# Attention and a mixture of experts in one program: the order of attention's work placed by a list of tasks

## The chip, the cores and the metric
The kernel runs on one core of a Trainium2 chip. The metric is the device time of one execution in microseconds (us). The core's engines are TensorE (PE in the profile, with its weight loads as PEld), VectorE (DVE), ScalarE (ACT), GpSimd (POOL) and SyncE (SP), which only issues transfers. Each engine runs its own queue of instructions strictly in order; an instruction waits in its queue until what it needs has been signalled by others, and everything behind it on that engine waits too.

## The reference
Attention with a bias that a small network computes from the positions, then a mixture of eight experts in which each token goes to its best expert.

```python
B, H, S, D = q.shape                      # 2, 8, 576, 64
scores = np.matmul(q, k.transpose(0, 1, 3, 2)) / np.sqrt(D)
x = (np.log1p(np.abs(rel)) / psi_i)[..., None]        # of the positions alone
bias = np.maximum(x @ w1 + b1, 0.0) @ w2              # hidden 32, one value per head
scores = scores + bias.transpose(2, 0, 1)[None]       # the same for both batches
attn = np.exp(scores - scores.max(-1, keepdims=True))
attn = attn / (attn.sum(-1, keepdims=True) + 1e-09)
x = np.matmul(attn, v)                    # laid out as 1152 tokens x 512
logits = x @ w_gate                       # 8 experts
# each token goes to its argmax expert, at most 288 tokens each, in order
y = np.maximum(x_e @ w1[e], 0.0) @ w2[e]  # 512 -> 1024 -> 512, for each expert
out[token] = gate_w[token] * y            # gate_w: softmax probability; 0 if not kept
```

## The kernel before
**Units.** Attention is cut into 40 units, numbered in the order in which they run. A unit is a batch, a tile t of query rows (t = 0 to 3 of 128 rows, t = 4 of 64) and a pair of heads; four units in a row make a tile. Batch 0 runs its tiles 4, 3, 2, 1, 0 (units 0 to 19), batch 1 its tiles 0 to 4 (units 20 to 39). For a unit, `scores` multiplies queries and keys on TensorE into two PSUM buffers `s`, one for each head (L211, L218 for t = 4). `softmax` adds the bias tile `bt` and takes the row minimum of the negated sum on VectorE (L223, output `ed`, minimum `mn`), then the exponential with its row sum on ScalarE (L227). Two units later (LAG = 2) `transp_rem` and `transp` turn the exponentials around on TensorE (L235): the last 64 columns (the remainder) into free corners of a later unit's `s`, the rest into the one PSUM buffer `tt`. Copies bring them to SBUF: the remainder `rt` (L266) and, in two halves, `at` (L248 on ScalarE, L250 on VectorE). `attn_v` (L289) multiplies them with the values into `av`. After a tile, `tile_a` copies `av` to `xT` (L303) and `tile_b` multiplies by a matrix that turns it back and applies the gate (L326), then scales by the row sums on VectorE (L329 to L346) and stores the rows `x` to DRAM.

**Bias blocks.** The bias is computed once, in 36 blocks of 16 query rows, for tiles 4, 3, 2, 1, 0 in turn. For each block, `hidden` makes four tiles `hid` (on VectorE L147, ScalarE L145 or GpSimd L143), `bias_block` multiplies them on TensorE (L166) into `tt`, `s` or `pt` and writes the block out of PSUM in two pieces, `bo` (L175 on VectorE, L177 on ScalarE). The block is stored to DRAM (L180, on SP's or ScalarE's queue) and read back skewed as bias tiles `bt`, of which four are kept (L193, L196, SP's queue). So batch 0's units run beside the bias blocks, batch 1's alone.

**Experts.** After batch 0 its tokens are routed (`group_a`, `group_b`, `pick`), and the first expert's rows of batch 0 are gathered (`match`, `fetch`, index products at L420). Its weights are loaded and split into a high and a low half (`wh` L85, L87, `wl` L90). `step(0, 0..9)`, its input transposes (L624) and eight halves of layer 1 (L633), are put between the units of batch 1. Layer 2 (L657), the second expert and a small part of a third follow attention.

**What sets the order.** One loop over slots n, a unit each, emits the program. TensorE's queue is the order of emission (`manual_schedule` with `MANF`). On the other engines a scheduler of the framework orders the instructions when the program is built, by its own estimates and priorities. In a slot, `attn_v` comes for two units at a time in every second slot, then two bias blocks, the scores, and the transposes:

```python
        for u in ([n - 4, n - 3] if n % 2 == 0 and 4 <= n <= NU else [NU - 2, NU - 1] if n == NU + 1 else []):
            attn_v(u)
        for z in range(2):
            bias_block()
            for c in range(4):
                hidden()
        new = scores(n) if n < NU else []
```

Which engine makes which hidden tile, bias output and transpose copy stands in tables, `P["h"]`, `P["e"]` and `P["t"]`; bias blocks with an odd number use `tt`.

## Time and profile before

| | |
|---|---|
| median of 3 runs | 352.01 us (351.0 to 352.93) |
| the profiled execution | 350.3 us |
| its span, first to last instruction | 348.3 us |
| TensorE busy | 273.7 us, 79% of the span |
| VectorE, ScalarE, GpSimd busy | 200.2, 169.2, 87.9 us |
| TensorE's granted clock, mean | 0.929 of full (2.4 GHz) |
| moved by DMA | 59.84 MB |

An engine's busy time counts the instructions that it executes, not the waits between them; a matmul that is held up inside a group counts as busy. The granted clock of a stretch is a mean over two levels, 2.4 and 1.2 GHz.

### The profile page before, as it was taken

How to read it: one execution, taken by the hardware profiler on the slowest of the kernel's cores; microseconds unless marked ns; L12 is line 12 of the kernel's file. 1: busy time of each engine (PE TensorE's matmuls, PEld its weight loads, DVE VectorE, ACT ScalarE, POOL GpSimd, SP SyncE). 2: the span in 40 equal slices, each digit the busy share in tenths (PEclk: the TensorE clock that was granted, in tenths of full speed). 3: DMA queues.
4: the chain of work that ended last, by engine and by line, in shares of the span. 5: the costliest groups of instructions: out<-in, count | busy, mean ns of one | idle time of the engine just before them, and what ended most of it. 6: DMA issues, size and time to landing. Idle time of an engine off the chain costs nothing.

```text
span 348.3 us, 7329 instructions
## 1 busy us (share of the span) xinstructions
PE 273.7 (79%) x2801; PEld 205.7 (59%) x2801; DVE 200.2 (57%) x625; ACT 169.2 (49%) x348; POOL 87.9 (25%) x79
## 2 busy tenths in 40 slices
PE   4795675767697788787886977898897969799891
PEld 2222343444355356565664755787777959799880
DVE  5897479566655444553669654366478586661010
ACT  4575546716546555445555455465432453651230
POOL 1359285126411010000000670122122240300031
PEclk9999899898969899999999896999998787999997
DMA  6999675741274229646645884252003799200011
GB/s 202 359 307 357 209 281 190 292 154 70 86 272 152 107 58 347 237 135 206 201 138 162 312 286 153 91 134 88 2 23 117 271 323 390 73 2 0 3 48 36
DMA packets 27627, 59.84 MB, mean 172 GB/s; under 512 B 3812, under 2 KB 5348, under 8 KB 27584
## 3 DMA queue, kind: packets, MB, share of 16 engines
q1 hardware_dynamic: 24384, 51.97, 44.4%
q10 hardware_dynamic: 2304, 4.84, 3.6%
q0 software_dynamic: 896, 2.47, 2.5%
q8 instruction: 24, 0.39, 0.5%
q14 instruction: 19, 0.16, 0.1%
HBM read 42.57 MB, written 16.99 MB: 171 GB/s over the span
## 4 chain that ended last, share of the span: by engine, by line
PE 34%; issue 17%; ACT 11%; DVE 11%; POOL 2%; POOLq 0%; ACTq 0%
PE av L289 10%; PE s L211 9%; ACT ed L227 6%; ACT at L248 4%; DVE ed L223 3%; PE tt L235 3%; PE pt L633 3%; PE tt L166 2%; PE pt L326 2%; POOL out_dram L643 1%; DVE rt L266 1%; PE pt L657 1%; DVE x L346 1%; PE pt L420 1%; PE s L218 1%
## 5 line engine op out<-in xcount | busy, mean ns | idle before, releaser
L227 ACT ACTIVATE ed<-ed,mn 128x576 f32<-128x576 f32 x72 | 55.3, 769 | 28.2 <-DVE mn L223 26.6
L143 POOL TENSOR_SCALAR hid<-c_u,nbv 128x304 f32<-128x304 f32 (+14 forms) x32 | 46.8, 1474 | 59.9 <-PE tt L166 31.6
L248 ACT COPY at<-tt 128x512 f32<-128x512 f32 x62 | 35.2, 575 | 53.8 <-PE tt L235 51.9
L211 PE MATMUL s<-kraw,q 64*128 64x288 f32 x256 | 51.2, 463 | 7.0 <-DVE mn L223 5.0
L289 PE MATMUL av<-at,vt 128*64 128x128 f32 (+1 forms) x576 | 45.0, 281 | 13.6 <-ACT at L248 7.7
L223 DVE CUSTOM_DVE_ANT_0 ed<-s,bt 128x576 f32<-128x576 f32 x72 | 51.5, 748 | 0.0
L147 DVE TENSOR_SCALAR hid<-c_u,c_v 128x496 f32<-128x496 f32 (+17 forms) x86 | 41.2, 532 | 17.0 <-PE tt L166 16.9
L289 PEld LDWEIGHTS av<-at,vt 128*64 128x64 f32 x576 | 35.8, 142 | 18.4 <-ACT at L248 10.0
L211 PEld LDWEIGHTS s<-kraw,q 64*128 64x128 f32 x256 | 27.5, 202 | 26.8 <-issue 11.1
L166 PE MATMUL tt<-hid,c_w2bd 128*32 128x512 f32 (+17 forms) x176 | 24.4, 532 | 18.9 <-ACT at L248 14.8
L266 DVE COPY rt<-s 128x64 f32<-128x64 f32 (+1 forms) x80 | 14.2, 216 | 36.3 <-PE s L235 35.0
L90 POOL TENSOR_TENSOR wl<-raw,wh 128x1024 fp32r<-128x1024 f32 x8 | 18.8, 2356 | 50.7 <-ACT wh L85 37.4
L85 ACT CAST wh<-raw 128x1024 fp32r<-128x1024 f32 x20 | 20.6, 1048 | 19.1 <-DMA raw<-in_w_dram 13.0
L235 PE MATMUL tt<-c_ident,ed 64*128 64x64 f32 x576 | 27.3, 230 | 2.5 <-DVE bo L175 0.8
L235 PEld LDWEIGHTS tt<-c_ident,ed 64*128 64x128 f32 x576 | 22.9, 143 | 8.5 <-ACT at L248 4.2
L633 PE MATMUL pt<-xh,wh 128*128 128x288 f32 x64 | 19.8, 309 | 5.5 <-ACT y L642 1.3
L145 ACT ACTIVATE hid<-c_u,c_v 128x528 f32<-128x528 f32 (+14 forms) x26 | 16.6, 673 | 14.9 <-PE tt L166 8.0
L90 DVE TENSOR_TENSOR wl<-raw,wh 128x1024 fp32r<-128x1024 f32 x16 | 19.5, 1219 | 6.0 <-ACT wh L85 6.0
L166 PEld LDWEIGHTS tt<-hid,c_w2bd 128*32 128x32 f32 x176 | 5.8, 114 | 28.0 <-ACT at L248 15.5
L657 PE MATMUL pt<-hh,wh 128*128 128x288 f32 x64 | 21.0, 329 | 0.0
L657 PE MATMUL pt<-hh,wl 128*128 128x288 f32 x64 | 20.5, 320 | 0.0
L657 PE MATMUL pt<-hl,wh 128*128 128x288 f32 x64 | 20.4, 319 | 0.0
(172 smaller groups left out, 503.9 us busy)
## 6 DMA issues: line engine op xcount, KB each, us to landing
bt<-bd SPq DMA_DIRECT2D x28, 576.0 KB, 5.1
raw<-in_w_dram SPq DMA_DIRECT2D x24, 512.0 KB, 4.9
bd<-bo SPq DMA_DIRECT2D x20, 295.5 KB, 2.6
bd<-bo ACTq DMA_DIRECT2D x16, 295.5 KB, 3.9
vt<-in_v_dram SPq DMA_DIRECT2D x8, 320.0 KB, 4.9
kraw<-in_k_dram SPq DMA_DIRECT2D x8, 288.0 KB, 5.6
bt<-bd SPq DMA_DIRECT2D x8, 288.0 KB, 4.4
out_dram<-y SPq DMA_DIRECT2D x3, 768.0 KB, 10.0
```

What stands on the lines that cost most here:

```text
L90: (nc.vector if eng[1] == "d" else nc.gpsimd).tensor_tensor(lo, raw, hi.bitcast(F32), op=ALU.subtract)
L143: nc.gpsimd.tensor_scalar(hid[:, :m], wu[:, :m], nbv[:, w:w + 1], None, op0=ALU.max)
L147: nc.vector.tensor_scalar(hid[:, :m], wu[:, :m], bvw[:, w:w + 1], 0.0, op0=ALU.add, op1=ALU.max)
L166: nc.tensor.matmul(ps[32 * c:32 * c + 32, lo:hi], lhsT=w2bd, rhs=hids[n, c][:, lo:hi], start=True, stop=True, tile_position=(0, 32 * c))
L211: nc.tensor.matmul(ps[i][:, r, :HALF], lhsT=q[p, hp], rhs=k[p, r * HALF:(r + 1) * HALF], start=True, stop=True, tile_position=(64 * i, 0))
L223: nc.vector.tensor_tensor_reduce(out=ed.rearrange("p (r j) -> p r j", r=2), in0=ps[:, :, :HALF], in1=bias.rearrange("p (r j) -> p r j", r= ...
L227: nc.scalar.activation(ed, ed, AF.Exp, scale=-1.0, bias=mn, accum_out=total)
L235: nc.tensor.transpose(out[r][:w], ed[p, o:o + w], ident[p, p], tile_position=(64 * r, 0))
L248: nc.scalar.copy(o, v)
L289: nc.tensor.matmul(o, lhsT=lh, rhs=rh, start=(j == 0), stop=(j == 4), tile_position=(0, r))
L633: nc.tensor.matmul(ph[:, :cap], lhsT=u[:, k], rhs=x[:, k], start=(k + z == 0), stop=(k == 3 and z == 2))
L657: nc.tensor.matmul(py[:, :cap], lhsT=w, rhs=hx, start=(f + i == 0), stop=(f == 7 and i == 2))
```

## The change
The loop over slots, the tables `P` and the calls at slots go. In their place attention, the routing and the first expert's part inside it are described as some 800 tasks. A task has the engines that may do it, a duration for each, the tasks that must end before, a rank, and the buffers that it takes with the tasks that give them back. `place_tasks` takes, of the tasks that can start first (or within 0.3 us of it), the one with the lowest rank, gives it the engine that ends it soonest and, where there is a choice, the PSUM buffer that is free soonest, and emits its instructions. All engines' queues now follow this order through attention. Behind it a short list, in the order of before, emits the rest, with TensorE alone in the order of emission.

To that end the functions are cut in pieces that are tasks of their own (matmul, output and store of a bias block; minimum and exponential; transposes and their copies; the pieces of `tile_b`, `group_a`, `group_b`, `pick` and layer 1). All bias stores go to SP's queue. Pools grow: `hid` from 13 to 16 buffers, `sm` from 3 to 4, `vr` from 2 to 4. In a bias block one hidden tile is always GpSimd's and another may be, and odd and even blocks share `pt` and `tt`.

```diff
-    hp_p = brest.enter_context(tc.tile_pool(name="hid", bufs=13, side="right"))
+    hp_p = brest.enter_context(tc.tile_pool(name="hid", bufs=HB, side="right"))
...
-    P = {
-        "h": ['daad', 'dddd', 'daad', 'daad', 'daad', 'dadp', 'dadp', 'dadd', 'dapp', 'daad', 'dddd',
...
-        "e": 'dadddaadaaadaaaddaadaaaddaadaadaadaa',
...
+    def bias_psum(n):
+        return ("s", "tt") if n < 4 else ("tt",) if span(blocks[n]) > 512 else ("pt", "tt")
...
+    def turned_rem(n, eng):
+        m = 128 if units[n][1] < 4 else 64
+        rt = ats[n, 1] = atp.tile([128, 128], F32, name="rt")
+        for r, z in enumerate(rps.pop(n)):
+            (nc.scalar.copy if eng == "a" else nc.vector.tensor_copy)(rt[:m, 64 * r:64 * r + 64], z[:m])
...
+    man = ExitStack()
+    man.enter_context(tc.manual_schedule(engines={ET.PE, ET.DVE, ET.Activation, ET.Pool, ET.SP}))
...
+    bufs = {"hid": HB, "bo": BB, "s": 2, "tt": 1, "pt": 1, "av": 1, "bt": 4, "q": 3, "v": 4, "vr": 4, "ed": 4, "at": 4,
+            "rt": 4, "mn": 4, "sums": 4, "xT": 2, "x": 2, "raw": 3}
+    after_us = {"e": 0.3, "d": 0.12, "a": 0.15, "p": 0.2, "s": 2.3}
...
+    def place_tasks(start):
+        free_at = dict(start)
+        ends, held, left = {}, {}, dict(tasks)
+        while left:
+            best = []
+            for name, (engines, us, fn, after, rank, takes, late) in left.items():
+                if any(a not in ends for a in after):
+                    continue
+                ready = max([ends[a] for a in after], default=0.0)
...
+                if len(chosen) == len(takes):
+                    e = min(engines, key=lambda e: (max(free_at[e], ready) + us[e], e))
+                    best.append((max(free_at[e], ready), rank, name, e, chosen))
+            first = min(b[0] for b in best)
+            at, rank, name, e, chosen = min((b for b in best if b[0] <= first + 0.3), key=lambda b: (b[1], b[0]))
...
+            free_at[e] = at + us[e]
+            ends[name] = at + us[e] + after_us[e] + late
...
+        for c in range(4):
+            engines = "p" if c == 3 and n >= 4 else "dap" if c == 2 and n >= 4 else "da"
+            task(("H", n, c), engines, {"d": 0.08 + m * 1.04e-3, "a": 0.25 + m * 0.9e-3, "p": m * 3.4e-3},
...
+        task(("S", n), "e", 1.1, (lambda n=n: scores(n)), after=src + [slot(n - 1)], rank=n - 0.5,
...
+        task(("T", n), "e", 0.55 if full else 0.32, (lambda n=n: transp(n)), after=[("R", n)], rank=n + LAG - 0.55,
+             takes=[("tt", [("C", n, i) for i in two(n)])])
...
+            task(("L", n, i), "d", 0.7, (lambda n=n, i=i: least(n, i)), after=[("S", n), bias] + rem, rank=n + 0.1 + 0.01 * i,
+                 takes=[("mn", [("X", n, i)])])
+            task(("X", n, i), "a", 0.8, (lambda n=n, i=i: expo(n, i)), after=[("L", n, i)], rank=n + 0.1 + 0.01 * i)
+            task(("C", n, i), "ad", {"a": 0.5, "d": 0.62}, (lambda e, n=n, i=i: turned(n, i, e)), after=[("T", n)] + [("C", n, 0)] * i,
+                 rank=n + LAG + 0.5, takes=[("at", [("V", n)])] if i == 0 else [])
+        task(("C", n, 2), "da", {"d": 0.3, "a": 0.5}, (lambda e, n=n: turned_rem(n, e)), after=[("R", n)], rank=n + LAG + 0.3, takes=[("rt", [("V", n)])])
...
+    place_tasks({"e": 5.0, "d": 4.6, "a": 4.6, "p": 5.5, "s": 4.5})
+    man.close()
+    man.enter_context(tc.manual_schedule(engines={ET.PE}))
...
-        for u in ([n - 4, n - 3] if n % 2 == 0 and 4 <= n <= NU else [NU - 2, NU - 1] if n == NU + 1 else []):
-            attn_v(u)
```

Three places show what moves. The first is TensorE's queue in stage 1, among the bias blocks of tile 2: before, from the bias block of 400 columns on (the pieces L166 are bias blocks, L211 scores, L235 transposes).

```order
L166 MATMUL tt<-hid,c_w2bd 32x400 x4
L166 MATMUL pt<-hid,c_w2bd 32x384 x4
L211 MATMUL s<-kraw,q 128x288 x4
L235 MATMUL s<-c_ident,ed 128x64 x2
L235 MATMUL tt<-c_ident,ed 128x64 x16
L166 MATMUL tt<-hid,c_w2bd 32x368 x4
L166 MATMUL pt<-hid,c_w2bd 32x352 x4
```

In the changed kernel the same place reads (L147 bias blocks, L201 scores, L233 transposes, L288 attention·V):

```order
L201 MATMUL s<-kraw,q 128x288 x4
L147 MATMUL tt<-hid,c_w2bd 32x400 x4
L233 MATMUL s<-c_ident,ed 128x64 x2
L288 MATMUL av<-at,vt 64x128 x8
L288 MATMUL av<-rt,vt 64x128 x2
L147 MATMUL pt<-hid,c_w2bd 32x384 x4
L233 MATMUL tt<-c_ident,ed 128x64 x16
L147 MATMUL pt<-hid,c_w2bd 32x368 x4
L201 MATMUL s<-kraw,q 128x288 x4
L147 MATMUL tt<-hid,c_w2bd 32x352 x4
```

Before, a bias block into tt stands right behind the transposes into tt; now one into pt and the next scores stand between them, and an attention·V stands alone.

The second is TensorE's queue in stage 2, two units of batch 0's last tile: before,

```order
L211 MATMUL s<-kraw,q 128x288 x4
L235 MATMUL s<-c_ident,ed 128x64 x2
L235 MATMUL tt<-c_ident,ed 128x64 x16
L211 MATMUL s<-kraw,q 128x288 x4
L235 MATMUL s<-c_ident,ed 128x64 x2
L235 MATMUL tt<-c_ident,ed 128x64 x16
L289 MATMUL av<-at,vt 64x128 x8
L289 MATMUL av<-rt,vt 64x128 x2
L289 MATMUL av<-at,vt 64x128 x8
L289 MATMUL av<-rt,vt 64x128 x2
```

and in the changed kernel, two units of batch 1's first tile:

```order
L201 MATMUL s<-kraw,q 128x288 x4
L233 MATMUL s<-c_ident,ed 128x64 x2
L288 MATMUL av<-at,vt 64x128 x8
L288 MATMUL av<-rt,vt 64x128 x2
L233 MATMUL tt<-c_ident,ed 128x64 x16
L201 MATMUL s<-kraw,q 128x288 x4
L233 MATMUL s<-c_ident,ed 128x64 x2
L233 MATMUL tt<-c_ident,ed 128x64 x16
L288 MATMUL av<-at,vt 64x128 x8
L288 MATMUL av<-rt,vt 64x128 x2
```

The pair of attention·V groups is split: one stands behind each unit's scores, before or behind its transposes.

The third is ScalarE's queue in stage 2 (L227 and L225 exponentials, L248 and L247 transpose copies): before,

```order
L227 ACTIVATE ed,sums<-ed,mn 128x576 x2
L248 COPY at<-tt 128x2x4x64 x2
L227 ACTIVATE ed,sums<-ed,mn 128x576 x2
L248 COPY at<-tt 128x2x4x64
L227 ACTIVATE ed,sums<-ed,mn 128x576 x2
L248 COPY at<-tt 128x2x4x64 x2
```

and now, with L265 the copy of the remainder:

```order
L265 COPY rt<-s 128x64 x2
L225 ACTIVATE ed,sums<-ed,mn 128x576 x2
L247 COPY at<-tt 128x2x4x64
L265 COPY rt<-s 128x64 x2
L225 ACTIVATE ed,sums<-ed,mn 128x576 x2
L247 COPY at<-tt 128x2x4x64 x2
```

The remainder's copies come over from VectorE, which takes some of the transpose copies instead. Over the whole program VectorE's hidden tiles go from 86 to 50, ScalarE's from 26 to 52, GpSimd's from 32 to 42; bias output pieces on VectorE from 28 to 54, on ScalarE from 44 to 18; transpose copies on VectorE from 10 to 28, on ScalarE from 62 to 44; remainder copies on VectorE from 80 to 12, on ScalarE from 0 to 68. Before unit 16 VectorE's remainder copies go from 30 to 12 and ScalarE's from 0 to 18, VectorE's transpose copies from 4 to 8 and ScalarE's from 21 to 16, VectorE's xT copies from 3 to 1 and ScalarE's from 0 to 2; all hidden tiles and bias outputs lie there.

## Rows read from the trace of the kernel before

**Rows 1.** The page's first part: busy time (us) of each engine, share of the span, number of instructions.
```profile
PE 273.7 (79%) x2801; PEld 205.7 (59%) x2801; DVE 200.2 (57%) x625; ACT 169.2 (49%) x348; POOL 87.9 (25%) x79
```

**Rows 2.** TensorE's timeline at the two cuts; columns: start, duration (us), engine, line, operation, output<-inputs, partitions, shape, count, in brackets the idle time before and what ended it.
```profile
134.59 1.24 PE L211 MATMUL s<-kraw,q 64*128 64x288 f32 x8
...
272.67 0.61 PE L657 MATMUL pt<-hh,wh 128*128 128x288 f32 x1
```

**Rows 3.** Busy time by stage; columns: stretch, its length, busy us (instructions) of PE, PEld, DVE, ACT and POOL, granted clock of TensorE, share of the DMA engines, GB/s.
```profile
0.00:134.59 134.59, 96.09 (x999) 53.88 (x999) 88.17 (x234) 72.94 (x147) 49.84 (x42) 0.92 0.62 212
134.59:272.73 138.14, 115.56 (x1371) 93.38 (x1369) 79.17 (x302) 65.67 (x148) 25.15 (x21) 0.95 0.50 162
272.73:348.30 75.57, 62.00 (x436) 58.47 (x435) 32.82 (x89) 30.62 (x53) 12.95 (x16) 0.91 0.35 119
```

**Rows 4.** Waits from 22.87, the scores of unit 0, to 134.59: who waited for whom, us in total, times, the longest.
```profile
DVE hid L147 <- PE tt L166: 16.9, 7, 3.3
...
PE tt L166 <- ACT at L248: 14.8, 5, 4.6
```

**Rows 5.** Timelines of TensorE, VectorE and ScalarE in one cycle of stage 1.
```profile
75.40 0.67 PE L235 MATMUL tt<-c_ident,ed 64*128 64x64 f32 x16
80.19 1.25 PE L166 MATMUL tt<-hid,c_w2bd 128*32 128x368 f32 x8 [4.12 <-ACT at L248]
...
74.08 1.07 DVE L175 TENSOR_SCALAR bo<-tt,c_rv,corr 128x400 f32<-128x400 f32 x2
...
78.61 0.68 DVE L250 COPY at<-tt 128x512 f32<-128x512 f32 x1
...
78.04 0.78 ACT L227 ACTIVATE ed<-ed,mn 128x576 f32<-128x576 f32 x1 [3.68 <-DVE mn L223]
...
79.57 0.56 ACT L248 COPY at<-tt 128x512 f32<-128x512 f32 x1
81.61 1.08 ACT L177 ACTIVATE bo<-tt,corr,c_rv 128x368 f32<-128x368 f32 x2 [1.48 <-issue]
```

**Rows 6.** TensorE's timeline in one cycle of stage 2.
```profile
151.40 1.09 PE L289 MATMUL av<-at,vt 128*64 128x128 f32 x16 [0.89 <-DVE x L346]
...
152.51 1.07 PE L289 MATMUL av<-at,vt 128*64 128x128 f32 x16
...
153.73 1.24 PE L211 MATMUL s<-kraw,q 64*128 64x288 f32 x8
154.80 0.22 PE L235 MATMUL s<-c_ident,ed 64*128 64x64 f32 x2
...
156.21 1.69 PE L211 MATMUL s<-kraw,q 64*128 64x288 f32 x7 [0.68 <-PE tt L235]
...
158.29 0.71 PE L235 MATMUL tt<-c_ident,ed 64*128 64x64 f32 x16
158.93 1.09 PE L289 MATMUL av<-at,vt 128*64 128x128 f32 x16
...
161.48 1.47 PE L289 MATMUL av<-at,vt 128*64 128x128 f32 x15 [1.23 <-ACT at L248]
...
163.20 1.24 PE L211 MATMUL s<-kraw,q 64*128 64x288 f32 x8
```

**Rows 7.** TensorE's timeline where the first expert's work lies between units: an input transpose and slow scores, the first and the next instruction after one half of layer 1, the second gather's index products.
```profile
210.95 0.74 PE L624 MATMUL pt<-c_ident,xe 96*128 96x96 f32 x3 [2.85 <-DVE xl L626]
211.62 2.29 PE L211 MATMUL s<-kraw,q 64*128 64x288 f32 x8
...
223.34 0.40 PE L633 MATMUL pt<-xh,wh 128*128 128x288 f32 x1
...
225.13 1.24 PE L211 MATMUL s<-kraw,q 64*128 64x288 f32 x8
...
267.54 2.27 PE L420 MATMUL pt<-tokv,match 128*96 128x6 bf16 x24
```

**Rows 8.** Busy time in two stretches of 20 us, with the columns of rows 3.
```profile
40.00:60.00 20.00, 14.13 (x201) 8.54 (x200) 15.93 (x42) 10.25 (x22) 13.43 (x10) 1.00 0.74 271
220.00:240.00 20.00, 18.87 (x227) 16.41 (x224) 11.30 (x39) 11.87 (x27) 3.31 (x3) 1.00 0.32 88
```

**Rows 9.** Groups of instructions by line, engine, operation and tile: count | busy us, mean ns of one | idle time before. The last row is that of one line: shortest, median and longest in ns.
```profile
L147 DVE TENSOR_SCALAR hid<-c_u,c_v 128x496 f32<-128x496 f32 (+17 forms) x86 | 41.2, 532 | 17.0 <-PE tt L166 16.9
L143 POOL TENSOR_SCALAR hid<-c_u,nbv 128x304 f32<-128x304 f32 (+14 forms) x32 | 46.8, 1474 | 59.9 <-PE tt L166 31.6 <-PE pt L166 23.1 <-PE s L166 5.2
L145 ACT ACTIVATE hid<-c_u,c_v 128x528 f32<-128x528 f32 (+14 forms) x26 | 16.6, 673 | 14.9 <-PE tt L166 8.0 <-DVE hid L147 4.0 <-DVE c_v L451 2.9
L266 DVE COPY rt<-s 128x64 f32<-128x64 f32 (+1 forms) x80 | 14.2, 216 | 36.3 <-PE s L235 35.0 <-PE s L211 1.3
L90 DVE TENSOR_TENSOR wl<-raw,wh 128x1024 fp32r<-128x1024 f32 x16 | 19.5, 1219 | 6.0 <-ACT wh L85 6.0
L227 ACT ACTIVATION_READ_ACCUMULATOR ed<-ed,mn 128x1 f32 x72 | 13.5, 187 | 0.0
L177 ACT ACTIVATE bo<-pt,corr,c_rv 128x79 f32<-128x79 f32 x1 | 0.4, 416 | 0.0
...
L147 DVE TENSOR_SCALAR hid<-c_u,c_v x86: 368/482/993, 4.9 to 110.9; 128x544 f32<-128x544 f32 x7, 128x496 f32<-128x496 f32 x7, 128x336 f32<-128x336 f32 x7, 128x384 f32<-128x384 f32 x7
```

More of the change, by code (lines that the diff above doesn't have):

```diff
@@ L201, in scores @@
         b, t, hp = units[n]
+        if t < 4:
+            sc = [big.tile([128, 2, 512], F32, name="s") for _ in range(2)]
         ed = eds[n] = ep.tile([128, 2, S], F32, name="ed")
@@ L206, in scores @@
         if t < 4:
-            ps = [big.tile([128, 2, 512], F32, name="s") for _ in range(2)]
+            ps = sc
             for r in range(2):
@@ L330, in tile_b @@
         else:
-            nc.tensor.matmul(ps[1][:64, 256:260], lhsT=ident[:, 64:128], rhs=sums[:, 0:4], start=True, stop=True)
             iv = inv.rearrange("p (a r) -> p r a", r=2)
@@ L454 @@
     nc.gpsimd.tensor_scalar(nbv, bvw, -1.0, 1.0, op0=ALU.mult, op1=ALU.mult)
-    for c in range(12):
-        hidden()
     pcor = pst.tile([128, 512], F32, name="pt")
@@ L897, with task @@
-    man.__exit__(None, None, None)
+    bufs = {"hid": HB, "bo": BB, "s": 2, "tt": 1, "pt": 1, "av": 1, "bt": 4, "q": 3, "v": 4, "vr": 4, "ed": 4, "at": 4,
+            "rt": 4, "mn": 4, "sums": 4, "xT": 2, "x": 2, "raw": 3}
+    after_us = {"e": 0.3, "d": 0.12, "a": 0.15, "p": 0.2, "s": 2.3}
+    tasks = {}
+    def task(name, engines, us, fn, after=(), rank=0.0, takes=(), late=0.0):
+        us = us if isinstance(us, dict) else {e: us for e in engines}
+        takes = [((p,) if isinstance(p, str) else p, users) for p, users in takes]
+        tasks[name] = (engines, us, fn, [a for a in after if a is not None], rank, takes, late)
@@ new lines @@
+    chain(("P", 2), "d", [0.8, 0.7, 0.5], pick(2), after=[("P", 1)], rank=36.0)
+    for z, nt in enumerate((5, 8)):
+        for j in range(nt):
+            task(("MT", z, j), "d", 0.42, (lambda z=z, j=j: match(z, j)), after=[("P", z), ("FE", z - 1) if z else None],
+                 rank=24.0 + 12 * z)
+    task(("FE", 0), "e", 1.2, lambda: fetch(0, X[0], 5), after=[("MT", 0, j) for j in range(5)] + ["pools"]
+         + [("BD", 0, t) for t in range(NT)], rank=25.0, takes=[("pt", [("FE", 0)])], late=6.0)
@@ new lines, with run @@
+    task("clear", "p", 1.0, lambda: nc.gpsimd.memset(X[0], 0.0), after=[("XM", k) for k in range(4)], rank=33.0)
+    task(("FE", 1), "e", 2.0, fetch1, after=[("MT", 1, j) for j in range(8)] + ["clear"] + [("BD", 1, t) for t in range(3)],
+         rank=38.0, takes=[("pt", [("FE", 1)])], late=6.0)
+    place_tasks({"e": 5.0, "d": 4.6, "a": 4.6, "p": 5.5, "s": 4.5})
+    man.close()
+    man.enter_context(tc.manual_schedule(engines={ET.PE}))
+    def run(gen):
+        for _ in gen or ():
+            pass
@@ new lines, with then @@
+    urgent = {tile_a, tile_b, tile_c, tile_d, group_a, group_b, group_c, rest_list, fetch2}
+    later = []
+    def then(f, *a):
+        later.append((f, a))
+    then(tile_a, 1, 4)
+    then(rest_pools)
+    then(fetch2)
+    then(step, 0, 10)
+    for f in (tile_b, tile_c, tile_d):
+        then(f, 1, 4)
+    then(group_a, 2)
+    for c in range(8):
+        then(weights, 1, c)
+    then(step, 0, 11)
+    then(group_b, 2)
+    then(group_c, 2)
+    then(step, 0, 12)
+    then(rest_list)
+    then(step, 0, 13)
@@ new lines @@
+    for i in range(8):
+        then(step, 1, i)
+    for c in range(4):
+        then(weights, 2, c)
+    for i in range(8, 12):
+        then(step, 1, i)
+    for c in range(4, 8):
+        then(weights, 2, c)
+    for i in range(12, 14):
+        then(step, 1, i)
+    for i in range(5):
+        then(small, i)
+    then(small, 5)
+    then(step, 1, 14)
+    then(small, 6)
+    for f, a in later:
+        if f in urgent:
+            with tc.high_priority():
+                run(f(*a))
+        else:
+            f(*a)
```

463 lines of the change are left out of this document (254 added, 209 removed).

## Prediction

> **What bounds the kernel now.** I read the split by engine first, then the same split by stage, then the waits of stage 1, and last the instructions of one cycle in each stage. Over the span no engine is full: TensorE 79%, VectorE 57%, ScalarE 49%, GpSimd 25% [rows 1]. I cut the span at two events: the first scores matmul of unit 16, at 134.59, after which no bias block is left, and the first layer 2 matmul of the first expert, at 272.67, which ends attention [rows 2]. In stage 1, up to the first cut, VectorE is busy 88.2 of 134.6 us, ScalarE 72.9, TensorE 96.1; in stage 2, between the cuts, TensorE is busy 115.6 of 138.1 us, part of it stretched by waits; the rest is 75.6 us [rows 3]. So attention, 272.7 of 348.3 us, is bound by no engine's work but by waits that come from the order in which work stands in the engines' queues.
>
> The waits of stage 1 name it: TensorE stands 14.8 us, in five pieces, for ScalarE's copies out of the one transpose buffer tt, and VectorE 16.9 us, in seven, for TensorE's bias matmuls [rows 4]. One cycle shows how [rows 5]. The transposes of a unit begin at 75.40. TensorE's next instruction is a bias block that wants tt again, so it stands until 80.19, idle for 4.12 us, though other work was ready. The copies that free tt come late: VectorE's stands behind bias outputs, hidden tiles and two minima and starts at 78.61, ScalarE's stands behind two exponentials, from 78.04, and starts at 79.57. The exponentials in turn waited for VectorE's minima. Each engine waits for the next.
>
> Stage 2 has no bias work and shows the same in small [rows 6]. From the scores at 153.73 to those at 163.20, 9.47 us for two units, TensorE is stopped 0.68 us before the second scores, held up inside them (1.69 us instead of 1.24) and stopped 1.23 us between the two attention·V groups, for ScalarE's copies.
>
> **The change part by part.** What a unit costs TensorE at the full clock, start to start [rows 6]: scores 1.07 us (153.73 to 154.80), transposes 0.64 (158.29 to 158.93), with the remainder's two 0.70, attention·V 1.11 (151.40 to 152.51).
>
> (1) The order of TensorE in stage 2. Its work there is 24 scores, 26 transposes and 26 attention·V: 25.7 + 18.2 + 28.9 us. With it come 8 halves of layer 1 at 1.79 (223.34 to 225.13), 14.3; 6 gate products of eight matmuls each, taken as eight of layer 1's twelve, 1.2, together 7.2; 4 input transposes at 0.67 (210.95 to 211.62), 2.7; the second gather's 24 index products, 2.3, and, at that rate, 52 small ones of the first gather and the prefix sums, 4.9 [rows 7]. Together 104 us, a stage of 138.1. The new order puts one attention·V, not two, between scores, and lets V and transposes alternate, so that the copies have a V or a scores to run behind. VectorE and ScalarE have less to do there than TensorE (part 4), so these 104 us are the floor. They are 75% of the stage now; where TensorE has layer 1 to fill its gaps it is busy 18.87 of 20 us, 94% [rows 8]. I take 86%, just above the middle: 121 us, 17 less.
>
> (2) Who does what in stage 1, counted from the two orders before unit 16. VectorE gives up 36 of 86 hidden tiles (41.2 us for 86: −17.2), 18 of 30 remainder copies (0.216: −3.9) and 2 xT copies (as large as a transpose copy, 0.68: −1.4), and takes 13 bias outputs (1.07 for the two pieces of one: +13.9) and 4 transpose copies (0.68: +2.7): 88.2 − 5.9 = 82.3 us [rows 3, 5, 9]. ScalarE takes 26 hidden tiles (16.6 us for 26 now: +16.6), 2 xT copies (+1.1) and the 18 remainder copies, and loses 13 bias outputs (1.08: −14.0) and 5 transpose copies (0.56: −2.8) [rows 5, 9]. GpSimd goes from 32 hidden tiles to 42 (1.474: +14.7), to 64.5 [rows 3, 9]. TensorE's own work stays.
>
> The remainder copy on ScalarE has no row. It lies between 0.187, ScalarE's smallest instruction, and 0.416, its copy of 79 columns out of PSUM [rows 9]. I take 0.40, near the second, which is the same operation: 7.2 us for the 18, so ScalarE comes to 72.9 + 16.6 + 1.1 + 7.2 − 14.0 − 2.8 = 81.0, with bounds of 77.2 and 81.3. [...]
>
> (3) Stage 1's length. VectorE, the fullest of three nearly equal engines, is busy 65.5% of it now, and in its best 20 us 80% [rows 3, 8]. With the copies, the minima and the bias work no longer in fixed groups I take 74%, again just above the middle: 82.3/0.74 = 111 us, 23.6 less.
>
> (4) In stage 2 VectorE loses 50 remainder copies (−10.8), takes 14 transpose copies (+9.5) and six low halves of weights from GpSimd (1.219: +7.3): 79.2 becomes 85. ScalarE loses 13 transpose copies (−7.3) and takes 50 remainder copies (+20): 65.7 becomes 78 [rows 3, 5, 9]. Both lie under 104 us and cost nothing while TensorE is the floor; without that cover VectorE would be next.
>
> (5) DMA. All bias stores now go through SP, 16 of them from ScalarE's queue, so that each transfer stands behind SP's wait for a bias output. Stage 1 moves 212 GB/s for 134.6 us, 28.5 MB; in 111 us that is 257 GB/s, and 271 is reached now [rows 3, 8]. I cost it at nothing: four bias tiles are kept, so a load has the minima of up to four units to hide behind; if they run out, a tile costs what it is late. Larger buffers take no engine time.
>
> (6) After attention TensorE's order stays; its 75.6 us [rows 3] are taken as they are.
>
> Sum, against the profiled execution's 350.3 us: 350.3 − 23.6 − 17 = 309.7. It lies 1.7 under the median of the runs, 352.01; I say 311.
>
> **The rivals.**
> *Half the packing.* The order now rests on durations written into the source; where one of them slips, all that stands behind it on that engine slips too. If packing stayed as it is, stage 1 would be 82.3/0.655 = 125.6 and stage 2 138.1: 341. Halfway to my case: 326. For it: the scores at 211.62 took 2.29 us after 2.85 us of idleness, against 1.24 at 153.73 [rows 6, 7], and the table has one figure for both. Against: its figures (scores 1.1, transposes 0.55, minimum 0.7, exponential 0.8) are near the rows at full clock.
>
> *Near the fullest engine.* Stage 1 at 80%, stage 2 at 94%: 103 + 111 = 214, or 292. The rows that reach these shares have much ready work; for most of the stage there is less.
>
> *GpSimd holds up VectorE.* 42 tiles of 1.474 cover 62 of 111 us. If each hidden tile on VectorE waited out the GpSimd instruction that it meets, 56% of 50 would lose 0.74 us: 21 us, VectorE 103, stage 1 140, 5 longer than now, in all 339. [...] The rows are against most of it: the 86 hidden tiles take 368 to 993 ns, with a median of 482 [rows 9], while GpSimd was busy 49.8 us in the same stage [rows 3].
>
> *No gain from the order*, only from the mix of engines: 341.
>
> *Slower: the clock.* TensorE's granted clock was 0.92 and 0.95 of full in stages 1 and 2 [rows 3], so at 1.2 GHz for 16% and 10% of them. Each microsecond of full-speed work done at 1.2 costs one more. Stage 2 has 104 us of it and little slack. If 40 us more than now ran low, the gain would be gone; if 60, it is 371. Against: the slow scores follow idleness [rows 7], and that shrinks.
>
> **How the numbers follow.** My case 58% (own range 298 to 324), near the fullest engine 11%, half 14%, GpSimd 5%, no gain from the order 6%, slower 6%. The range from 292 to 334 leaves out half of the second, and the last three: about 2 in 10. Faster by more than 0.5%, about what a measurement here can tell from no change: all but the last and a little of the one before, 0.90; same 0.03; slower 0.07.
>
> **What would show it.** Right: scores of unit 16 near 111, layer 2 near 232, no idleness of 4 us on TensorE ahead of a bias block, VectorE near 74% in stage 1, TensorE busy about 90% of stage 2, granted clock above 0.95, about 75 us after layer 2 begins. Wrong: minima waiting for bias tiles, hidden tiles on VectorE well over 0.5 us, TensorE waiting for the first expert's rows or weights in the midst of units, remainder copies on ScalarE longer than 0.42, or a longer end.

## The result, and the profile after

The changed kernel takes 323.46 us (median of 4 runs, 320.56 to 328.79) beside 352.47 for the kernel before on the same chip: ratio 0.916, 95% interval 0.909 to 0.923. A later repetition gave 323.61 and a ratio of 0.929 (0.922 to 0.937), with the kernel before scattering from 347 to 357. Below, times are medians over all runs in us, while each ratio compares the faster runs alone, as some runs of either kernel are a per cent or two longer. The gain is 29 us; the forecast was 41, with 323 inside its range of 292 to 334.

The stages, cut at the same events as before: the first scores of unit 16 (106.50) and the first layer 2 matmul (250.53). First the page's engine line, then busy time by stage with the columns of [rows 3].

```profile
PE 268.0 (83%) x2801; PEld 202.6 (63%) x2801; DVE 205.6 (64%) x568; ACT 171.8 (53%) x401; POOL 87.2 (27%) x83
```

```profile
0.00:106.50 106.50, 83.66 (x959) 46.14 (x959) 81.26 (x198) 71.92 (x158) 60.27 (x51) 0.98 0.73 248
106.50:250.50 144.00, 124.84 (x1416) 100.47 (x1416) 93.39 (x290) 70.42 (x193) 17.19 (x21) 0.88 0.52 166
250.50:321.30 70.80, 59.54 (x430) 55.96 (x429) 30.92 (x81) 29.44 (x52) 9.72 (x12) 0.95 0.37 133
```

Against [rows 3]: stage 1 lost 28.1 us, more than forecast; stage 2, where 17 were to go, **grew** by 5.9, at a clock of 0.88 instead of 0.95; the rest lost 4.8. So the whole gain, and more, comes from stage 1. TensorE's idleness falls there by 15.7 us (38.5 to 22.8) and its busy time by 12.4, at a clock of 0.98 instead of 0.92. Two attention·V, 2.2 us, are part of the latter: the new order has them behind the cut (1416 instructions in stage 2, 1371 before).

What went there: TensorE's timeline over one cycle of stage 1 (columns of [rows 5]).

```profile
66.04 0.88 PE L147 MATMUL tt<-hid,c_w2bd 128*32 128x400 f32 x8
...
67.06 1.09 PE L288 MATMUL av<-at,vt 128*64 128x128 f32 x16
...
68.30 0.85 PE L147 MATMUL pt<-hid,c_w2bd 128*32 128x384 f32 x8
69.08 0.71 PE L233 MATMUL tt<-c_ident,ed 64*128 64x64 f32 x16
70.52 0.83 PE L147 MATMUL pt<-hid,c_w2bd 128*32 128x368 f32 x8 [0.73 <-DVE bo L160]
71.28 1.24 PE L201 MATMUL s<-kraw,q 64*128 64x288 f32 x8
72.45 0.80 PE L147 MATMUL tt<-hid,c_w2bd 128*32 128x352 f32 x8
```

Behind the transposes at 69.08 come a block into pt and scores, and only at 72.45 a block into tt, without a wait. In [rows 5] that block stood 4.12 us. Ahead of bias blocks TensorE waited 14.8 us for ScalarE's copies out of tt [rows 4] and 3.2 for VectorE's, which the first row below adds from the kernel before; in the groups of those matmuls 0.2 us are left, and the blocks into pt wait 4.7 for bias outputs (columns of [rows 9]).

```profile
PE tt L166 <- DVE at L250: 3.2, 1, 3.2
```

```profile
L147 PE MATMUL pt<-hid,c_w2bd 128*32 128x432 f32 (+12 forms) x152 | 17.1, 512 | 4.9 <-DVE bo L160 4.7
L147 PE MATMUL tt<-hid,c_w2bd 128*32 128x512 f32 (+11 forms) x136 | 13.6, 482 | 0.7 <-DVE bo L160 0.4 <-DVE at L249 0.2
...
L265 ACT COPY rt<-s 128x64 f32<-128x64 f32 (+1 forms) x68 | 11.2, 212 | 36.0 <-DVE mn L218 27.2 <-PE s L233 7.2 <-PE tt L233 1.2
```

The remainder copy on ScalarE, which had no row before, takes 212 ns.

Part of this may be the choice of buffer and not the order. In the kernel before the block behind the transposes had to take tt. In the cycle of [rows 5] the other buffer, pt, was read out by 76.1, 4 us before that block started:

```profile
75.06 1.07 DVE L175 TENSOR_SCALAR bo<-pt,c_rv,corr 128x384 f32<-128x384 f32 x2
```

The changed kernel takes pt at this place. What the free choice of buffer and the larger pools alone would bring, no run shows.

Where stage 2 went: TensorE at the end of attention and behind it, VectorE beside it, and the clock of three stretches.

```profile
225.73 0.41 PE L319 MATMUL av<-idwg,xT 128*128 128x144 f32 x2
231.05 0.32 PE L233 MATMUL s<-c_ident,ed 64*64 64x64 f32 x2 [4.91 <-ACT ed L225]
...
241.94 0.44 PE L674 MATMUL pt<-xl,wh 128*128 128x288 f32 x1
242.18 0.44 PE L674 MATMUL pt<-xh,wl 128*128 128x288 f32 x1
...
255.47 0.29 PE L707 MATMUL pt<-hh,wl 128*128 128x288 f32 x1
255.60 0.29 PE L707 MATMUL pt<-hh,wh 128*128 128x288 f32 x1
```

```profile
224.75 1.22 DVE L626 TENSOR_TENSOR wl<-raw,wh 128x1024 fp32r<-128x1024 f32 x1
...
226.96 2.46 DVE L442 TENSOR_SCALAR match<-iota,key,base 128x288 bf16<-128x288 f32 x7
229.34 0.74 DVE L218 CUSTOM_DVE_ANT_0 ed<-s,bt 128x576 f32<-128x576 f32 x1
```

```profile
180.00:225.70 45.70, 42.55 (x509) 35.24 (x508) 31.97 (x100) 24.12 (x70) 2.31 (x6) 1.00 0.34 103
225.70:250.50 24.80, 17.49 (x160) 15.10 (x158) 12.51 (x45) 5.01 (x13) 3.47 (x4) 0.59 0.19 57
228.70:249.10 20.40, 16.57 (x148) 14.43 (x149) 8.24 (x30) 4.64 (x13) 3.47 (x4) 0.50 0.15 45
```

The last two units' minima start at 229.34, 8 us after their scores (those of unit 39 start at 221.05). In VectorE's queue the choice of the next experts, a weight split and the second gather's match tiles stand ahead of them. TensorE waits 4.91 us for the exponentials. Behind that wait matmuls of 288 columns take 0.44 us and start 0.24 apart, where at 255.47, at a clock of 1.00, they take 0.29 and start 0.13 apart. The stretch has 0.59 of full clock, and 0.50 from 228.7 to 249.1; from 180 to 225.7, before it, TensorE was busy 93% at 1.00. A second place of this kind lies between 169.97 and 174.16, where input transposes wait 3.6 us for the gathered rows; but there the clock is low before the wait, too (0.66 from 160 to 170, with TensorE busy throughout).

### The profile page after: what moved, and what is told of

The parts are those of the page before. It is cut to its first block, busy times and chain, and to the rows that moved or that the text cites. A ratio compares the mean times of both kernels' runs of the same rounds, so it can differ in the third digit from the quotient of the medians.

```text
span 321.3 us, 7361 instructions
## 1 busy us (share of the span) xinstructions
PE 268.0 (83%) x2801; PEld 202.6 (63%) x2801; DVE 205.6 (64%) x568; ACT 171.8 (53%) x401; POOL 87.2 (27%) x83
## 5 line engine op out<-in xcount | busy, mean ns | idle before, releaser
L128 POOL TENSOR_SCALAR hid<-c_u,nbv 128x400 f32<-128x400 f32 (+17 forms) x42 | 59.0, 1417 | 29.3 <-PE tt L147 14.5
L225 ACT ACTIVATE ed<-ed,mn 128x576 f32<-128x576 f32 x72 | 55.8, 776 | 15.8 <-DVE mn L218 14.6
L201 PE MATMUL s<-kraw,q 64*128 64x288 f32 x256 | 46.5, 439 | 4.3 <-ACT rt L265 3.1
L288 PE MATMUL av<-at,vt 128*64 128x128 f32 (+1 forms) x576 | 45.4, 291 | 2.4 <-DVE x L361 1.6
L288 PEld LDWEIGHTS av<-at,vt 128*64 128x64 f32 x576 | 35.8, 149 | 9.1 <-issue 2.8
L201 PEld LDWEIGHTS s<-kraw,q 64*128 64x128 f32 x256 | 25.9, 190 | 17.2 <-ACT rt L265 4.6
L130 ACT ACTIVATE hid<-c_u,c_v 128x528 f32<-128x528 f32 (+17 forms) x52 | 31.4, 659 | 7.8 <-PE tt L147 4.1
L233 PE MATMUL tt<-c_ident,ed 64*128 64x64 f32 x576 | 27.9, 237 | 3.3 <-DVE bo L160 1.7
L265 ACT COPY rt<-s 128x64 f32<-128x64 f32 (+1 forms) x68 | 11.2, 212 | 36.0 <-DVE mn L218 27.2
L233 PEld LDWEIGHTS tt<-c_ident,ed 64*128 64x128 f32 x576 | 23.1, 147 | 10.9 <-issue 4.8
L247 ACT COPY at<-tt 128x512 f32<-128x512 f32 x44 | 24.1, 581 | 6.7 <-PE tt L233 3.9
L132 DVE TENSOR_SCALAR hid<-c_u,c_v 128x544 f32<-128x544 f32 (+17 forms) x50 | 25.1, 543 | 0.0
L147 PE MATMUL pt<-hid,c_w2bd 128*32 128x432 f32 (+12 forms) x152 | 17.1, 512 | 4.9 <-DVE bo L160 4.7
L160 DVE TENSOR_SCALAR bo<-pt,c_rv,corr 128x192 f32<-128x192 f32 (+31 forms) x32 | 17.1, 576 | 5.4 <-DMA bd<-bo 3.4
L674 PE MATMUL pt<-xl,wh 128*128 128x288 f32 x64 | 20.4, 318 | 0.0
L674 PE MATMUL pt<-xh,wl 128*128 128x288 f32 x64 | 20.0, 312 | 0.0
```

Of the source, the lines that this page charges most:

```text
L128: nc.gpsimd.tensor_scalar(hid[:, :m], wu[:, :m], nbv[:, w:w + 1], None, op0=ALU.max)
L130: nc.scalar.activation(hid[:, :m], wu[:, :m], AF.Relu, bias=bvw[:, w:w + 1])
L132: nc.vector.tensor_scalar(hid[:, :m], wu[:, :m], bvw[:, w:w + 1], 0.0, op0=ALU.add, op1=ALU.max)
L201: nc.tensor.matmul(ps[i][:, r, :HALF], lhsT=q[p, hp], rhs=k[p, r * HALF:(r + 1) * HALF], start=True, stop=True, tile_position=(64 * i, 0))
L225: nc.scalar.activation(ed, ed, AF.Exp, scale=-1.0, bias=mns.pop((n, i)), accum_out=total)
L233: nc.tensor.transpose(out[r][:w], ed[p, o:o + w], ident[p, p], tile_position=(64 * r, 0))
```

## The experiments

Each run was timed beside the kernel before, whose medians were 351.2 to 353.2. The changed kernel's repetition (e9) starts layer 2 at 248.92 instead of 250.53 and has a clock of 0.90 in stage 2 instead of 0.88, and its ten runs in both sets reach from 320.6 to 328.9; smaller differences than these rest on the waits in the traces.

**e1: what stands ahead of the last minima.** Ranks alone change (`MT`: match tiles, `P` 2: choice of the third expert, `WH`, `WO`: weight splits).

```diff
-    chain(("P", 2), "d", [0.8, 0.7, 0.5], pick(2), after=[("P", 1)], rank=36.0)
+    chain(("P", 2), "d", [0.8, 0.7, 0.5], pick(2), after=[("P", 1)], rank=41.0)
...
-                 rank=24.0 + 12 * z)
+                 rank=24.0 + 15.2 * z)
...
-             after=[("WL", c)] + wait, rank=28.0 + c)
+             after=[("WL", c)] + wait, rank=28.0 + c + (c > 5) * 6)
...
-             rank=28.5 + c)
+             rank=28.5 + c + (c > 5) * 6)
```

> The changed kernel with other ranks for what VectorE did ahead of the last two minima: the eight match tiles of the second gather, the choice of the third expert and the weight chunks 6 and 7. Theory A (the list itself places a wait at the end of attention, and the low clock behind it is its consequence): the 4.9 us of idleness on TensorE at 226 shrink below 1.5, the clock of the stretch from there to layer 2 (0.5 now, 24 us) rises, and with about 9 us of matmul time given back the time is 323.5 - 4 - 8 = about 311. Theory B (the idleness goes, the clock falls all the same): 319. Theory C (TensorE's work is the floor and the wait only moves): 323.

Measured: 318.23 (317.37 to 320.51), 5.3 less than the changed kernel's 323.5. TensorE's timeline and the clock of the stretch:

```profile
225.96 1.00 PE L319 MATMUL pt<-idwg,xT 128*128 128x144 f32 x6 [0.93 <-DVE hl L681]
...
228.87 0.47 PE L233 MATMUL tt<-c_ident,ed 64*128 64x64 f32 x8 [1.12 <-ACT at L247]
```

```profile
226.00:244.80 18.80, 15.60 (x163) 13.55 (x163) 11.12 (x45) 5.48 (x13) 5.83 (x5) 0.73 0.25 75
```

The 4.91 us are gone, waits of 0.93 and 1.12 remain, and layer 2 starts at 244.77, 5.8 earlier. The clock rose only to 0.73. The stretch is 6.0 us shorter, 4.1 of it idleness and 1.9 busy time: theory B in kind, the wait was real and the list had placed it, but its removal gave little clock back.

**e2: the true length of the first gather.** In the changed kernel its three instructions on GpSimd lie between 162.24 and 167.20, 5.0 us, and gathers of rows take 7.1 us from issue to landing (median of the program's seven).

```diff
-         + [("BD", 0, t) for t in range(NT)], rank=25.0, takes=[("pt", [("FE", 0)])], late=6.0)
+         + [("BD", 0, t) for t in range(NT)], rank=25.0, takes=[("pt", [("FE", 0)])], late=0.8)
+    task(("FG", 0), "p", 5.0, lambda: None, after=[("FE", 0)], rank=25.0, late=7.0)
...
-        task(("XM", k), "e", 0.45, (lambda k=k: x_mm(X[0], k, NB)), after=[("FE", 0)], rank=27.0 + k, takes=[("pt", [("XL", k)])])
+        task(("XM", k), "e", 0.45, (lambda k=k: x_mm(X[0], k, NB)), after=[("FG", 0)], rank=27.0 + k, takes=[("pt", [("XL", k)])])
```

> The changed kernel with the first gather given its true length in the table: 5 us on GpSimd and 7 us of transfer instead of 6 us behind the matmuls. Theory A (the 3.6 us that TensorE stands for the gathered rows between 170 and 174, and the low clock around them, are lost by a wrong figure): these waits go, 3.6 us and up to 2 of clock, 318 to 320. Theory B (layer 1 comes later and leaves more of it bare behind the last units, as the list's own sum says with 2 us more at the end): 323 to 326.

Measured: 320.47 (317.94 to 324.45). The input transposes now stand later, behind scores, without a wait for rows:

```profile
176.36 1.38 PE L201 MATMUL s<-kraw,q 64*128 64x288 f32 x8
177.67 0.47 PE L654 MATMUL pt<-c_ident,xe 96*128 96x96 f32 x3
...
179.66 0.44 PE L654 MATMUL pt<-c_ident,xe 96*128 96x96 f32 x3 [0.82 <-DVE xl L662]
```

Layer 2 starts at 246.86, 3.7 earlier, as theory A has it for the wait alone; the time, 3 us less, lies just above its 318 to 320, so little of the clock came back. The runs overlap those of the changed kernel; that the waits are gone is what the trace shows.

**e3: six buffers for bias outputs.** All orders stay.

```diff
-    HB, BB = 16, 4
+    HB, BB = 16, 6
```

> The changed kernel with 6 buffers instead of 4 for bias outputs; the order on every engine stays as it is. Theory A (the slip of 8 us against the list's own times that is there by unit 4 comes from bias outputs that wait for the store of an older one, 5.7 us on ScalarE and 3.4 on VectorE around 26): the wait goes, unit 4 starts some 4 us earlier and all behind it too, 319.5. Theory B (the queue of transfers is full there, and the minima wait for their bias tiles instead): 323.5.

Measured: 319.70 (317.72 to 323.48). ScalarE around 25, first the changed kernel, then e3:

```profile
28.26 1.09 ACT L162 ACTIVATE bo<-tt,corr,c_rv 128x112 f32<-128x112 f32 x2 [5.68 <-DMA bd<-bo]
29.24 0.77 ACT L225 ACTIVATE ed<-ed,mn 128x576 f32<-128x576 f32 x1
```

```profile
22.63 1.09 ACT L162 ACTIVATE bo<-tt,corr,c_rv 128x112 f32<-128x112 f32 x2 [0.33 <-PE tt L147]
25.08 0.78 ACT L225 ACTIVATE ed<-ed,mn 128x576 f32<-128x576 f32 x1 [1.37 <-DVE mn L218]
```

A bias output waited 5.68 us for the store of an older one, and behind it on ScalarE the first unit's exponential, for which TensorE waited. Without it unit 4 starts 4.8 us earlier (32.5 instead of 37.3) and layer 2 3.9 (246.6): theory A.

**e4: only TensorE in the list's order.**

```diff
-    man.enter_context(tc.manual_schedule(engines={ET.PE, ET.DVE, ET.Activation, ET.Pool, ET.SP}))
+    man.enter_context(tc.manual_schedule(engines={ET.PE}))
```

> The changed kernel with only TensorE's queue held to the list's order through attention; the order of VectorE, ScalarE, GpSimd and SyncE is left to the framework's scheduler as in the kernel before, while the engine of each task stays as the list chose it. Theory A (the gain comes from all queues following one order): half of it or more is lost, 337 or above. Theory B (TensorE's order and the mix of engines bring the gain): 323 to 327.

Measured: 326.66 (324.02 to 331.76), 3.2 more than the changed kernel: theory B. One order for all queues is worth about 1% in sum, hardly more than the runs scatter (e7 parts it into two effects); TensorE's order, with the engines and buffers chosen for it, brings the rest.

**e5 and e6: the order without the mix, the mix without the order.** e5 writes the changed kernel's engine for each task into the tables of the kernel before; e6 holds the list's tasks to the engines of those tables.

The cores of both, first e5's, with the tables `h`, `t` and the weights' changed likewise, then e6's, with the other tasks held likewise:

```diff
-        "e": 'dadddaadaaadaaaddaadaaaddaadaadaadaa',
+        'e': 'adaddddadaddddddddddaaadddddddadaddd',
...
-            nc.vector.tensor_copy(rt[:m, 64 * r:64 * r + 64], pr[r][:m])
+            (nc.scalar.copy if P["r"][n] == "a" else nc.vector.tensor_copy)(rt[:m, 64 * r:64 * r + 64], pr[r][:m])
```

```diff
-            engines = "p" if c == 3 and n >= 4 else "dap" if c == 2 and n >= 4 else "da"
+            engines = MIX_H[n][c]
...
-        task(("C", n, 2), "da", {"d": 0.3, "a": 0.5}, (lambda e, n=n: turned_rem(n, e)), after=[("R", n)], rank=n + LAG + 0.3, takes=[("rt", [("V", n)])])
+        task(("C", n, 2), "d", {"d": 0.3, "a": 0.5}, (lambda e="d", n=n: turned_rem(n, e)), after=[("R", n)], rank=n + LAG + 0.3, takes=[("rt", [("V", n)])])
```

> The kernel before, its loop over slots and its scheduler untouched, with the changed kernel's engine for every hidden tile, bias output, transpose copy, remainder copy, xT copy and weight half. Theory A (the order is the gain; the mix alone is worth 5.9 us of VectorE at the old packing, 9 us at most): 342 to 352, and TensorE's waits for copies out of tt stay near 15 us. Theory B (the mix is the gain): 330 or below.

> The changed kernel with each of these tasks held to the engine that it has in the kernel before; the list places them anew. Theory A (order and mix belong together: with the old mix the list's own sum puts unit 16 at 108 instead of 97 and the last attention V at 249 instead of 228): 340 to 345. Theory B (the order alone is enough, the list overprices VectorE's remainder copies, 0.3 us against 0.216 in rows 9): 330 or below.

Measured: e5 351.58 (ratio 1.004, 0.997 to 1.010), e6 336.99 (332.31 to 338.12; ratio 0.959, 0.937 to 0.981). The new mix in the old order gains nothing; the new order with the old mix gains about 15 us, by its interval 7 to 22; both together 29. e6 keeps the larger pools and the free choice between pt and tt, e5 has neither, so they count here with the order. In e5's profiled execution (span 353.3) TensorE still waits 14.0 us for copies out of tt (columns of [rows 4]), where it was 14.8 and 3.2, 18.0 in all:

```profile
PE tt L163 <- ACT at L245: 7.1, 4, 2.7
PE tt L163 <- DVE at L247: 6.9, 2, 3.7
```

e6 fell between its two theories: the order with its buffers is worth about half by itself, and the list's own sum, which put the last attention·V 21 us later with the old mix, overprices the mix: 337.0 less 323.5 is 13.5.

**e7: the list's order for all queues only up to unit 16.**

```diff
+            if name == ("S", 16):
+                man.close()
+                man.enter_context(tc.manual_schedule(engines={ET.PE}))
```

> The changed kernel with all queues in the list's order up to the scores of unit 16 and only TensorE's from there to the end of attention. Theory A (in stage 1 the order of all queues pays, in stage 2 the list's order of VectorE and ScalarE costs, as the match tiles ahead of the last minima do): stage 1 stays at 106 to 107, stage 2 falls from 144 to 136 to 139, 316 to 319 in all. Theory B (the list's order is better in both, or equal): 323 or above.

Measured: 317.14 (315.95 to 320.46). Stage 2 took 136.6 us (111.1 to 247.7), as theory A has it; stage 1 ended at 111.1, not 106 to 107. In this execution, the longest of the six, TensorE's busy time there is 3.4 us longer (87.1 against 83.7; the other microsecond is open), as the clock fell in its midst:

```profile
84.91 3.20 PE L201 MATMUL s<-kraw,q 64*128 64x288 f32 x8
88.04 1.98 PE L288 MATMUL av<-at,vt 128*64 128x128 f32 x16
```

Scores take 1.24 and attention·V 1.09 otherwise. By the medians, and as e4 differs from e7 in stage 1 alone, the list's order of the other queues is worth 9.5 us there (326.7 less 317.1); beside the changed kernel it costs 6.4 in stage 2 (323.5 less 317.1; by the traces 5.5 to 7.4, as stage 2 takes 144.0 or, in e9, 142.1).

**e8: the three waits at once.** The edits of e1, e2 and e3, and for the second gather's matmuls:

```diff
-         rank=38.0, takes=[("pt", [("FE", 1)])], late=6.0)
+         rank=42.0, takes=[("pt", [("FE", 1)])], late=0.8)
```

> The three changes of e1, e2 and e3 at once, and the second gather's matmuls behind layer 1's last two halves in the list (they hold the one buffer pt for less time in the table, too). Theory A (the three waits lie in different places and add up: layer 2 starts at 250.5 - 5.8 - 3.7 - 3.9 = 237): 309 to 312. Theory B (what is gained early is waited for at the end, for the last weights or the gather): 315 or above.

Measured: 312.55 (310.05 to 318.32; ratio 0.895, 0.885 to 0.905), 11 us below the changed kernel: nearly theory A. Stages, and TensorE's largest wait behind attention:

```profile
0.00:104.20 104.20, 84.28 (x958) 46.67 (x958) 81.48 (x198) 71.95 (x158) 59.83 (x51) 0.98 0.74 254
104.20:235.20 131.00, 117.17 (x1416) 93.61 (x1417) 94.50 (x291) 71.31 (x192) 17.52 (x20) 0.97 0.58 185
235.20:310.80 75.60, 60.77 (x429) 57.65 (x428) 30.95 (x80) 28.82 (x52) 12.91 (x15) 0.91 0.36 122
```

```profile
PE pt L404 <- DVE oh L386: 6.4, 1, 6.4
```

Layer 2 starts at 235.2, 15.3 earlier, more than the 13.4 of the three runs summed. The stage's clock is 0.97, and TensorE's busy time is 7.7 us shorter for the same matmuls: here the clock came back, though a part of the low clock has moved behind the cut, where the rest has 0.91 instead of 0.95. The rest is 4.8 us longer again: TensorE now stands 6.4 us for the routing of the last tiles, where it stood 2.7.

**e9, e10, e11: how much rests on the durations.** e9 is the changed kernel again. e10 multiplies each duration by a factor of its own, e11 makes them equal on each engine.

First e10's edit, then e11's:

```diff
+        k = sum((i + 1) * ord(z) for i, z in enumerate(str(name))) % 7
+        us = {e: v * (0.7 + 0.1 * k) for e, v in us.items()}
```

```diff
+        us = {e: {"e": 0.8, "d": 0.6, "a": 0.65, "p": 1.5, "s": 0.45}[e] for e in us}
```

> The changed kernel as it is, once more beside the next two. 0.916 of the time before, 321 to 324, stage 1 at 106 to 107, layer 2 at 249 to 251.

> The changed kernel with each task's duration in the table multiplied by a factor between 0.7 and 1.3 that depends on its name; the list places them by these wrong figures. Theory A (the gain rests on the table's durations, the prediction's rival of half the packing): 335 or above. Theory B (ranks, buffers and what waits for what make the order, and queues that wait in order take up errors of this size): 319 to 328.

> The changed kernel with one duration for all tasks of an engine in the table: 0.8 on TensorE, 0.6 on VectorE, 0.65 on ScalarE, 1.5 on GpSimd, 0.45 on SyncE. Theory A (the durations make the gain): 340 or above. Theory B (any figure near the mean does): 320 to 330.

Measured: 323.61 (321.41 to 328.85), 322.80 (318.67 to 325.17) and 321.37 (320.32 to 323.23): theory B for both. Their orders are not that of the changed kernel: about a fifth of VectorE's and ScalarE's instructions stand elsewhere (443 and 454 of VectorE's 568 keep their sequence, 319 and 328 of ScalarE's 401), so it is not one order alone that wins. Neither run touches the figures for what follows a task's end, such as the 6 us of the gather. In e11 the scores of unit 16 start at 105.6 and layer 2 at 248.9, as with the written durations (106.8 and 248.9 in e9).

**e12: the routing ahead of the weights.** e8, with the second expert's weights behind `group_c` in the closing list and VectorE, too, in that list's order.

```diff
-    for c in range(8):
-        then(weights, 1, c)
     then(step, 0, 11)
     then(group_b, 2)
     then(group_c, 2)
+    for c in range(8):
+        then(weights, 1, c)
...
-    man.enter_context(tc.manual_schedule(engines={ET.PE}))
+    man.enter_context(tc.manual_schedule(engines={ET.PE, ET.DVE}))
```

> The kernel of e8 with VectorE, too, held to the order of the list behind attention, and the second expert's eight weight chunks behind the routing of the last tiles in it. In e8 layer 2 starts 15.3 us earlier than in the changed kernel, the end comes only 10.5 earlier: TensorE stands 6.35 us for the routing's one-hot tile, whose chain on VectorE alternates with low halves of weights that wait for ScalarE and the transfer. Theory A (that order costs the 5 us): the wait falls below 1.5 us, 307 to 309. Theory B (the weights are what is late, and the second expert's layer 1 waits for them instead): 312 or above.

Measured: 314.83 (310.02 to 319.21; ratio 0.886, 0.877 to 0.894), not to be told from e8. TensorE's waits behind attention:

```profile
PE pt L674 <- DVE xl L662: 4.4, 1, 4.4
```

The 6.4 us are gone, and the second expert's layer 1 waits 4.4 for its inputs, whose low halves now stand behind the weight splits and the choice of the next expert on VectorE: theory B.

## Why the prediction was right, and where not

- **What bounds the kernel: right, in stage 1.** Waits from the order, not an engine's work. e5 shows it best: the lighter load on VectorE, its fullest engine beside TensorE, gains nothing while the old order, with its fixed buffers, stands.
- **Part 3, stage 1: right, a little short.** 111 forecast, 106.5 measured; VectorE is busy 81.3 us (82.3 counted), 76% (74% chosen). Split up, the working is less good: it let the mix alone give 9 us and the order the rest. e5 gives the mix 0, e6 the order 15, and the two are worth more together. The tt wait was named right, and the new order removes it, together with the choice of buffer. The working also divides the time of VectorE, although TensorE was the fuller engine (96.1 us) and is (83.7, 79%); that TensorE's own time would shrink by 12.4 us, with the clock going from 0.92 to 0.98, it did not count.
- **Part 1, stage 2: wrong, and it is the step that failed.** The choice of 86% gave 121; measured were 144, and 104 of 144 is 72%, no better than before. The 104 us hold only as a lower bound, and the share was not read from anything in the new order. Three things, which overlap, make up most of the difference. Two are waits that the list itself places: the last minima behind match tiles and weights (e1: layer 2 5.8 earlier) and too short a figure for the gather (e2: 3.7). The third is the clock: it was to pass 0.95 and fell to 0.88. With the waits gone (e8) the stage takes 131.0 at 0.97, with 5.4 us less idleness and 7.7 less busy time. The 10 us that still separate it from 121 lie in TensorE's busy time, 117.2 instead of 104, not in idleness, 13.8, where 17 had been allowed. The count took 26 attention·V, and 28 lie there: 2.2 us. Part of the rest is matmuls held up inside a group, as scores in the changed kernel from 139.91 to 142.06, 2.15 us with two remainder transposes among them, where scores alone took 1.07:

```profile
139.91 0.75 PE L201 MATMUL s<-kraw,q 64*128 64x288 f32 x2 [0.66 <-ACT rt L265]
140.83 0.99 PE L201 MATMUL s<-kraw,q 64*128 64x288 f32 x5 [0.17 <-DVE mn L218]
...
141.66 0.40 PE L201 MATMUL s<-kraw,q 64*128 64x288 f32 x1
```

- **Part 2, the remainder copy on ScalarE: mis-sized.** 0.40 taken, 0.212 measured, near the lower bound: 3.8 us for the 18 of stage 1 instead of 7.2, which is 3.4 of the 9.1 us by which ScalarE's 71.9 stays under my 81.0; another 1.8 is that its 52 hidden tiles take 31.4 us, not 33.2. The row that I chose, a bias output of 79 columns, does more than a copy.
- **Part 4: no cost while TensorE is fullest; right for the averages, wrong for the order.** VectorE's 93.4 of 144 us (85 counted) and ScalarE's 70.4 (78) hide, but its match tiles and the moved weight splits stood where the last minima were due.
- **Part 5, DMA at nothing: wrong by about 4 us** (e3). What ran out was not bias tiles, as I had it, but the buffers of bias outputs.
- **Part 6, the rest at 75.6: it took 70.8,** at a clock of 0.95 instead of 0.91. e8 and e12 show why it isn't a constant: when attention ends earlier, routing and the second expert's weights are late instead. Why it was 4.8 us shorter in the changed kernel no run shows.
- **The sum: in the range partly by luck.** Stage 2 took 23 us more than the 121 forecast. That 323 is only 12 over 311 comes from stage 1, 4.5 us better, and from the rest, 4.8, of which the prediction expected nothing.
- **The rivals.** *Half the packing* came near in time (326), by another cause: e10 and e11 show that wrong durations cost nothing that can be measured, save one for a transfer (e2). *GpSimd holds up VectorE*: the mechanism is there, at a quarter of its price. I read the median of [rows 9] as evidence against it, and the median hides it (492 ns against 482): tiles of 560 columns take 497 ns on average, those of 544 take 743. In the changed kernel 18 of VectorE's 50 hidden tiles are more than a tenth longer than others of their size, and all 18 run beside a hidden tile of GpSimd; together that is some 5 us, an estimate from the tiles that met none. In the kernel before it was 27 of 86 and some 8 us, so the change lessens it. Others meet GpSimd and are not longer, and no minimum passes 759 ns. The trace bears out a hold-up, but not that a tile waits out the GpSimd instruction that it meets: the longest, at 70.97, ends 0.6 us before the GpSimd tile beside it.

```profile
L132 DVE TENSOR_SCALAR hid<-c_u,c_v x50: 360/492/998, 5.8 to 97.1; 128x544 f32<-128x544 f32 x4, 128x560 f32<-128x560 f32 x4, 128x576 f32<-128x576 f32 x4, 128x384 f32<-128x384 f32 x4
L218 DVE CUSTOM_DVE_ANT_0 ed<-s,bt x72: 741/757/759, 24.6 to 230.0; 128x576 f32<-128x576 f32 x72
...
L132 DVE TENSOR_SCALAR hid<-c_u,c_v 128x544 f32<-128x544 f32 x4 | 2.8, 743 | 0.0
L132 DVE TENSOR_SCALAR hid<-c_u,c_v 128x560 f32<-128x560 f32 x4 | 1.8, 497 | 0.0
...
70.93 1.68 POOL L128 TENSOR_SCALAR hid<-c_u,nbv 128x560 f32<-128x560 f32 x1
70.97 1.00 DVE L132 TENSOR_SCALAR hid<-c_u,c_v 128x576 f32<-128x576 f32 x1
```

- *The clock* rival had the right mechanism in stage 2 at a smaller size: at most 7.7 us of busy time between 0.88 and 0.97 (e8), not the 40 at which the gain would be gone. In stage 1 the clock went the other way and added to the gain.

## What to carry to other kernels

Here the list placement won by the order that follows from its ranks, buffers and dependences. Errors of up to 30% in its durations cost nothing that could be measured; a rank out of place cost 5 us, and a transfer entered at about half its length some 3. So the time to spend on such a list goes to ranks, and to buffers, first. Look in the new order for cheap side work that stands ahead of the last instructions on the path, above all near the end of a stage, before a busy share is assumed for that stage. Taking work off the fullest engine gained nothing while another engine's queue stood in order behind a wait (e5: 351.58 us, ratio 1.004). A median over tiles of many sizes can hide that some of them are twice as long as others: compare tiles of one size.
